# Attention and a gated feed-forward on one core: sums of exponentials on VectorE, turns of 32-bit pairs, and a new order for every engine

## The chip, the cores and the metric

The kernel runs on one NeuronCore of a Trainium2 chip. Five engines work on their own instruction queues, each in order: TensorE (PE in the profile, with its weight loads as PEld), VectorE (DVE), ScalarE (ACT), GpSimd (POOL) and SyncE (SP). In this kernel POOL only issues the loads and SP the stores. The metric is the device time of one launch in microseconds; less is better. The time before is 416.05 us, the median of three runs.

## The reference

Attention over 8 batches of 12 heads, 448 tokens, head size 64, and then a feed-forward with one gate over all 3584 tokens:

```
scores = (q @ k^T) / sqrt(64)                     # 8 x 12 x 448 x 448
attn   = softmax(scores)
x      = (attn @ v), heads side by side           # 3584 x 768
h      = x @ w_in                                 # 3584 x 2048
out    = (h * sigmoid(h)) @ w_out                 # 3584 x 768, float32
```

The inputs are float32 in memory; the loads turn them into fp16 on the way.

## The kernel before

**Units of attention.** Four heads make a group, three groups a batch. A unit is one group with a range of queries: batch 0 is cut into two pieces of queries (7 blocks of 32 each), so it has 6 units of 224 queries, and each later batch has 3 units of 448: 27 units. For each unit, `load_k`, `load_q` and `load_v` fetch fp16 tiles; `turn_k` (L265) and `turn_q` (L287) transpose 32x32 blocks on VectorE, so that 32 numbers of a head lie on 32 partitions. A head has 64 numbers, so there are two such halves (`e` = 0 and 1): the first and the last 32 numbers.

**Scores and exponentials.** The keys are cut into four chunks. `scores` (L315) makes one burst for one chunk: four heads work at the same time in four row strips of 32 of the array, and the two halves `e` add up in PSUM. `expo` (L335) makes exponentials on ScalarE, two heads at a time, into an fp16 tile `E`. The softmax has no subtraction of the maximum. The first seven units stand alone; the 20 others go in pairs, where the fourth chunk of both units has 64 keys each and shares one burst (`scores_rest`, L324) and one tile `E`.

**Columns.** `attend` (L364) multiplies the exponentials with V in four column strips of 32, one for each head, and it runs three times for a unit or a pair. Part 0 multiplies with `ones` and so gives the sums of the exponentials, that is, the denominators; parts 1 and 2 multiply with the first and the last 32 numbers of V. In a pair each part streams three chunks of each unit and then the shared fourth chunk. `inverse` (L387) turns the sums, takes reciprocals and turns them back, and `norm` (L403) multiplies and writes `xT`, the input of the feed-forward.

**Feed-forward.** `ffn1` (L420) multiplies `xT` with 16 blocks of w_in; `tanh` on ScalarE and `gate` (L464) on VectorE make the gated value (the sigmoid is had from the tanh of half the value). For the second product, two tiles of 128 tokens make a quad that is multiplied with seven products in place of eight; their inputs are sums of halves, made on VectorE by `combine_w` (L452) for the weights, once, and by `combine_g` (L489) for the tokens, in two halves of four blocks. `product` (L508) runs them, and `take_1` to `take_7` and `less_12`, `less_21` put the results together. The first two tiles of tokens are multiplied in the `plain` way (L524). `store` (L552) writes each output tile with four transfers, from SP, and a part of the last from ScalarE.

**What sets the order.** The program is written out by a planner in the kernel's own code: class `Order` (L76) keeps an estimated time and, for PE, ScalarE, VectorE and POOL, when each is free; every operation has an estimated length, dependencies and a bias. ScalarE and VectorE take the ready operation with the least sum of ready time and bias. PE's choice is made in the loop at L1082: a score burst when it is due (at most one per `PACE`, 2.6 us), else a column burst or a feed-forward product. Buffers are rings (`Ring`, L32): 2 score tiles of two PSUM banks, 4 other PSUM banks, 9 tiles `E`, 18 tiles `xT`, 6 output tiles and so on. `load` (L110) gives the loads in a fixed order; L652 to L677 list it. Until the first product, PE fills waits with multiplications of zeros (`run_zeros`, L1073). The estimates only set the order; on the chip every engine goes through its queue in that order and waits for what it needs.

Of the kernel before, what the change touches and what calls it, by code (L numbers as in the profile page):

```python
# [10 lines left out]
FP32 = mybir.dt.float32  # L11
AF = mybir.ActivationFunctionType
# [7 lines left out]
DMA_RATE = 0.37  # L20
DMA_TAIL = 1.0
# [54 lines left out]
class Order:  # L76


    def __init__(self):
        self.now = 0.0  # L80
        self.free = {"PE": 1.2, "ACT": 2.1, "DVE": 1.2, "POOL": 1.2}
        self.wait = {"ACT": [], "DVE": []}
        self.pool = []
        self.dma_free = 0.0
        self.out = []
        self.mode = None
        self.busy = {e: 0.0 for e in self.free}
# [22 lines left out]
    def load(self, mb, emit, ring=None, gate=None):  # L110
        op = Op("POOL", 0.58, emit)
        self.pool.append((op, mb, ring, gate))
        return op

    def step(self):

        soon = []
        for eng in ("ACT", "DVE"):
# [3 lines left out]
            best = None  # L122
            for op in self.wait[eng]:
                at = op.ready()
                if at is None:
                    continue
                if at > self.now:
                    soon.append(at)
                elif best is None or at + op.bias < best[0]:
                    best = (at + op.bias, op)  # L130
            if best:
                self.wait[eng].remove(best[1])
                self.start(best[1])
                soon.append(self.free[eng])
        if self.free["POOL"] > self.now:
            soon.append(self.free["POOL"])
        elif self.pool:
            op, mb, ring, gate = self.pool[0]
# [3 lines left out]
            if at is not None and gate is not None:  # L142
                g = gate()
                at = None if g is None else max(at, g)
            if at is not None and at <= self.now:
# [4 lines left out]
                self.dma_free = max(self.dma_free, self.now + 1.5) + mb / DMA_RATE  # L150
                op.done = self.dma_free + DMA_TAIL
                soon.append(self.free["POOL"])
# [6 lines left out]
def kernel(  # L159
# [31 lines left out]
    NE, NXT = 9, 18  # L191
    NSG, NTMP, NOST = 3, 3, 6
# [24 lines left out]
    pS_t = {}  # L217
# [4 lines left out]
    def load_k(b, hg):  # L222
        t = sb.tile([128, TPP, 2, 32], FP16, name=f"rk_{b}_{hg}", tag="rk", bufs=2)
        nc.gpsimd.dma_start(out=t, in_=group_of(k, b, hg))  # L224
        rawk[(b, hg)] = t

    def load_q(n):
        b, hg, g0, g1 = units[n]
        t = sb.tile([128, g1 - g0, 2, 32], FP16, name=f"rq_{n}", tag="rq", bufs=3)
# [21 lines left out]
    def load_w_in(h, j, f0, f1):  # L251
        src = moe_w_in.rearrange("(c h j p) f -> h j p c f", h=HG, j=2, p=32)
        dst = w_in_t.rearrange("p (c j) f -> p j c f", j=2)
        nc.gpsimd.dma_start(  # L254
            out=dst[32 * h : 32 * (h + 1), j, :, f0:f1], in_=src[h, j, :, :, f0:f1]
# [9 lines left out]
    def turn_k(b, hg, e):  # L265
        t = rawk[(b, hg)]
        if e == 0:
            KT[(b, hg)] = sb.tile(
                [128, 2, NCH, 4, 32], FP16, name=f"KT_{b}_{hg}", tag="KT", bufs=3
            )  # L270
        kt = KT[(b, hg)]
        toks = X_TOK[form(b, hg)]
        x = 0
        while x < 4:
            first, count = toks[x]
            y = x + 1
            while y < 4 and toks[y][1] == count:
                y += 1
            nc.vector.transpose(  # L279
                out=kt[:, e].rearrange("p c x i -> p x c i")[:, x:y, 0:count],  # L280
                in_=t[:, first : first + count * (y - x), e, :].rearrange(
# [5 lines left out]
    def turn_q(n):  # L287
        b, hg, g0, g1 = units[n]
        qt = sb.tile([128, 2, g1 - g0, 32], FP16, name=f"QT_{n}", tag="QT", bufs=3)
        nc.vector.transpose(out=qt.rearrange("p e g i -> p g e i"), in_=rawq[n])  # L290
        QT[n] = qt
# [7 lines left out]
    def score(pS, n, c, e, h, x0, x1, p0):  # L299
# [5 lines left out]
            lhsT=KT[(b, hg)][32 * h : 32 * (h + 1), e, c, x0:x1, :],  # L305
            rhs=QT[n][32 * h : 32 * (h + 1), e],
# [41 lines left out]
    def attend_mm(a, n, part, c, h, k0, k1, e, start, stop):  # L348
# [5 lines left out]
        else:  # L354
            w = VT[b][k0:k1, HG * hg + h, c, 32 * (part - 1) : 32 * part]
# [8 lines left out]
    def attend(ns, part):  # L364
        made = []
        lone = len(ns) == 1
        for n in ns:
            a = ps.tile([128, 512], FP32, name=f"a_{n}_{part}", tag="m", bufs=4)
            made.append(a)
            acc[(n, part)] = a  # L370
            for c in range(NCH if lone else NCH - 1):
                for h in range(HG):
                    attend_mm(
                        a, n, part, c, h, 0, rows_of(n, c), E[(n, c // per_burst(n))],
                        c == 0, lone and c == NCH - 1,
                    )
        if not lone:
            for h in range(HG):
                for i, n in enumerate(ns):
                    attend_mm(  # L380
                        made[i], n, part, 3, h, 64 * i, 64 * (i + 1), E[(ns[0], 3)],
                        False, True,
                    )


# [138 lines left out]
    def plain(t, j):  # L524
        o = ps.tile([128, 512], FP32, name=f"o_{t}_{j}", tag="m", bufs=4)
        pr_t[("o", t, j)] = o
        for f in range(NFF):
# [81 lines left out]
    s_ring, m_ring, e_ring = Ring(2), Ring(4), Ring(NE)  # L609
    rk_ring, rq_ring, v_ring = Ring(2), Ring(3), Ring(2)  # L610
    kt_ring, qt_ring = Ring(3), Ring(3)
    ld_k, ld_q, ld_v, ld_win, ld_wout = {}, {}, {}, {}, {}
    kt_op, qt_op, exp_op, rdn_op, x_op, g_op = {}, {}, {}, {}, {}, {}
    last_unit = {(u[0], u[1]): n for n, u in enumerate(units)}
    MB = 1e-6 * 4 * 32 * HG * D

    def plan_k(b, hg):
        ld_k[(b, hg)] = od.load(1.2 * MB * TPP, lambda: load_k(b, hg), rk_ring)

    def plan_q(n):  # L620
        ld_q[n] = od.load(1.2 * MB * (units[n][3] - units[n][2]), lambda: load_q(n), rq_ring)

    def plan_v(b, hg0, hg1):
        made = []
        for x in range(4):
            ring = v_ring if (x == 0 and hg0 == 0) else None
            mb = MB * (hg1 - hg0) * X_TOK[form(b, hg0)][x][1]
            made.append(od.load(mb, lambda x=x: load_v(b, hg0, hg1, x), ring))
# [3 lines left out]
    def plan_w_in(f0, f1):  # L632
        made = [
            od.load(4e-6 * 96 * (f1 - f0), lambda h=h, j=j: load_w_in(h, j, f0, f1))
            for h in range(HG)
            for j in range(2)
# [4 lines left out]
    def plan_w_out(half):  # L641
        made = []
        for f in range(0, NFF, 4):
            made.append(
                od.load(
                    4e-6 * 512 * OH,
# [5 lines left out]
    for hg in range(NG):  # L652
        plan_k(0, hg)
        plan_q(hg)
    plan_v(0, 0, NG)
    NB0 = NG * len(PIECES)
    for n in range(NG, 2 * NG):
        plan_q(n)
    plan_w_in(0, DFF // 4)
    for n in range(2 * NG, NB0):  # L660
        plan_q(n)
    plan_w_in(DFF // 4, DFF // 2)
    plan_k(1, 0)
    plan_q(NB0)
    plan_w_in(DFF // 2, DFF)
    plan_k(1, 1)
    plan_q(NB0 + 1)
    plan_w_out(0)
    plan_k(1, 2)
    plan_q(NB0 + 2)  # L670
    for hg in range(NG):
        plan_v(1, hg, hg + 1)
    plan_w_out(1)
# [15 lines left out]
    def plan_turn(n):  # L689
        b, hg, g0, g1 = units[n]  # L690
        if (b, hg) not in kt_op:
# [3 lines left out]
            for e in range(2):  # L695
                op = Op("DVE", 0.72, lambda e=e: turn_k(b, hg, e), [ld_k[(b, hg)]], 20)
                if e == 1:
                    op.then = rk_ring.give
                kt_op[(b, hg)] = od.add(op)
        if not qt_ring.can(1, od.now):  # L700
            return False
        qt_ring.take()
        busy = 0.1 + (g1 - g0) * 64 / 960.0
        qt_op[n] = od.add(
            Op("DVE", busy, lambda: turn_q(n), [ld_q[n]], 20, then=rq_ring.give)
# [8 lines left out]
    inv_op, norm_op = [], []  # L714
    quads = []

    def queue_ffn1(b, g0, g1):
        t0, t1 = 32 * g0, 32 * g1
        for f in range(NFF) if b == 0 else [x for f in range(HF) for x in (f, f + HF)]:

            def run(f=f):
                op = Op("PE", NDC * mm(t1 - t0), lambda: ffn1(b, f, t0, t1), tail=PE_OUT)
                if warm["on"]:
# [5 lines left out]
                    Op("ACT", act(t1 - t0), lambda: tanh(b, f, t0, t1), [op], -0.3, tail=0.2)  # L729
# [6 lines left out]
                    -4,  # L736
                    then=m_ring.give,
                )
                g_op.setdefault((b, f), []).append(od.add(g))
                ffn1_left[b] -= 1  # L740
# [17 lines left out]
    def sums_w(ms):  # L758

        for m in ms:  # L760
# [7 lines left out]
                        30,  # L768
# [5 lines left out]
    def queue_plain(t, j):  # L774
        def run():
            op = Op("PE", NFF * mm(OH), lambda: plain(t, j), tail=PE_OUT)
            m_ring.take()
            od.on_pe(op, "full")
            plain_op[(t, j)] = op
            od.add(  # L780
                Op("ACT", act(OH), lambda: take_plain(t, j), [op], -2, then=m_ring.give)
            )
            if len(plain_op) == 4:
                sums_w((3, 7))

        def deps():
            if any(len(g_op.get((0, f), ())) < len(PIECES) for f in range(NFF)):
                return [None]
            return ld_wout[j] + [(x, f * mm(OH)) for f in range(NFF) for x in g_op[(0, f)]]

        moe.append((deps, 1, run))
# [6 lines left out]
    def plan_sums():  # L798
# [12 lines left out]
        for m in (5, 2, 1, 6, 7):  # L811
            sg_op[(qd, m)] = []
            for f0 in (0, 4):
                deps = [x for f in range(f0, f0 + 4) for x in gates[f] + gates[f + HF]]
                if m > 5:
                    deps += sg_op[(qd, {6: 2, 7: 5}[m])]
                sg_op[(qd, m)].append(
                    od.add(
                        Op(
                            "DVE",  # L820
                            0.34,
                            lambda m=m, f0=f0: combine_g(qd, m, f0, f0 + 4),
                            deps,
                            0,
                        )
                    )
                )

    def queue_quad(qd):
# [3 lines left out]
        def read(m, eng, fn, deps, then=None):  # L833
            busy = act(OH) if eng == "ACT" else OH / 960.0 + 0.13
            bias = -2 if eng == "ACT" else -4
            took[m] = od.add(Op(eng, busy, lambda: fn(qd), deps, bias, then=then))

        def queue(m, first):
# [25 lines left out]
            def deps():  # L864
# [10 lines left out]
                x = sg_op.get((qd, m), [None, None])  # L875
                return made + [x[0], (x[1], 4 * mm(OH))]
# [47 lines left out]
    for ns in jobs:  # L924
        if len(ns) == 1:
            split = ((0,), (1,)) if ns[0] < 6 else ((0, 1),)
# [6 lines left out]
    av_data = {"at": None}  # L933

    def qk_at():
# [9 lines left out]
        if at is None or s is None or e is None:  # L945
            return None
        return max(at, s, e)

    def run_qk():
        ns, c, ys = qk_seq.pop(0)  # L950
        n = ns[0]
# [20 lines left out]
        for y in ys:  # L972
# [10 lines left out]
            for m in ns:  # L983
                exp_op.setdefault(m, []).append(made)
# [174 lines left out]
```

## Time and profile before

| | |
|---|---|
| runs | 414.36, 416.05 and 422.96 us; median 416.05 |
| span of the profiled execution | 414.8 us (the page gives no other time for it) |
| TensorE busy | 402.2 us, 97% of the span; granted clock 0.998 of full speed |
| weight loads, beside the matmuls | 208.0 us |
| VectorE, ScalarE busy | 285.2 us, 233.2 us |
| GpSimd busy (it issues the loads) | 95.8 us |
| moved by DMA | 34.46 MB |

An engine's busy time is the union of its instructions' times. Matmuls overlap, since the next one enters the array before the last one has left it, so one of 448 columns shows 353 ns where a row of them goes on every 0.188 us or so. In the chain that ended last, pieces are merged: "x12" are twelve matmuls, and the number before the engine is the time that they took on the chain. In a list of waits the three numbers are the total in us, how often, and the longest. In a list of groups the numbers after the count are the busy time in us and the mean of one in ns, and then the idle time before them and what ended it.

### The profile page before, as it was taken

Reading aid. Unit: us, or ns where it says so; the run is one execution under the profiler, and the core shown is the slowest. Engines: PE = TensorE matmul, PEld = TensorE weight load, DVE = VectorE, ACT = ScalarE, POOL = GpSimd, SP = SyncE. Lnnn points to the kernel's source line nnn. Section 1 sums busy time; section 2 is a strip of 40 time slices with the busy share of each in tenths; the row PEclk is TensorE's granted clock in tenths of the full one; section 3 lists DMA queues with packets and bytes.
Section 4 is the critical chain, followed back from the end, with each engine's and each line's share of the span. In section 5 each row is a group of like instructions: output and inputs, shape, how many; then the busy total and the mean of one; then the engine's idle time right before and its main releaser. Section 6 shows DMA issues by size and latency. Waiting matters only on the chain.

```text
span 414.8 us, 9788 instructions
## 1 busy us (share of the span) xinstructions
PE 402.2 (97%) x3939; PEld 208.0 (50%) x3939; DVE 285.2 (69%) x654; ACT 233.2 (56%) x360; POOL 95.8 (23%) x175
## 2 busy tenths in 40 slices
PE   8999999899999999999999899999999999999994
PEld 8676765344454445544445444444445444555562
DVE  3556765899868477867868838949577557684763
ACT  2987884587365794058476197476683373314410
POOL 6685374723000810053100071403000000000000
PEclk9999999999999999999999999999999999999999
DMA  6999999954313960284402294365002300032014
GB/s 102 147 169 193 203 131 210 197 79 69 50 40 92 128 92 14 60 135 77 73 3 57 72 154 72 35 109 92 1 6 51 81 19 2 22 81 54 0 45 108
DMA packets 38749, 34.46 MB, mean 83 GB/s; under 512 B 11952, under 2 KB 37936, under 8 KB 38704
## 3 DMA queue, kind: packets, MB, share of 16 engines
q0 software_dynamic: 27952, 22.82, 38.2%
q1 hardware_dynamic: 10560, 10.83, 10.3%
q8 instruction: 31, 0.51, 0.5%
q10 hardware_dynamic: 192, 0.20, 0.2%
q14 instruction: 14, 0.11, 0.1%
HBM read 45.61 MB, written 11.01 MB: 136 GB/s over the span
## 4 chain that ended last, share of the span: by engine, by line
PE 79%; DMA 10%; DVE 6%; POOL 3%; issue 1%; ACT 0%; DVEq 0%
PE h L423 32%; PE p L514 27%; PE a L356 10%; PE s L303 8%; DMA rq<-in_q_dram 6%; DMA rk<-in_k_dram 3%; PE z L1077 2%; DMA w_in_t<-in_moe_w_in_dram 1%; POOL w_in_t L254 1%; DVE sT L392 1%; DVE KT L279 1%; POOL V L243 1%; DVE QT L290 1%; DVE rdn L401 1%; DVE xT L409 1%
## 5 line engine op out<-in xcount | busy, mean ns | idle before, releaser
L340 ACT ACTIVATE E<-s 128x896 f16<-128x896 f32 (+1 forms) x172 | 148.4, 914 | 54.3 <-PE s L303 53.3
L423 PE MATMUL h<-xT,w_in_t 128*128 128x448 f16 (+1 forms) x864 | 157.5, 333 | 2.5 <-DVE xT L409 1.5
L423 PEld LDWEIGHTS <-w_in_t 128*128 128x128 f16 x864 | 79.1, 98 | 75.8 <-issue 22.0
L470 DVE SCALAR_TENSOR_TENSOR G<-th,h 128x448 f16<-128x448 f16 (+2 forms) x144 | 74.9, 530 | 55.6 <-ACT th L434 52.6
L434 ACT ACTIVATE th<-h 128x448 f16<-128x448 f32 (+1 forms) x144 | 71.5, 506 | 55.6 <-PE h L423 47.3
L243 POOL DMA_DIRECT2D V<-in_v_dram x88 | 48.6, 564 | 127.6 <-PE a L356 108.5
L303 PE MATMUL s<-QT,KT 32*128 32x448 f16 (+4 forms) x864 | 54.3, 334 | 1.7 <-ACT E L340 1.1
L514 PEld LDWEIGHTS <-G 128*128 128x128 f16 x384 | 36.5, 98 | 29.3 <-issue 5.7
L514 PEld LDWEIGHTS <-S 128*128 128x128 f16 x312 | 29.3, 98 | 23.2 <-issue 4.3
L356 PE MATMUL a<-E,V 128*32 128x448 f16 (+3 forms) x864 | 40.5, 335 | 0.0
L279 DVE STREAM_TRANSPOSE KT<-rk 128x256 f16<-128x256 f16 (+2 forms) x96 | 31.6, 377 | 12.0 <-DMA rk<-in_k_dram 10.3
L514 PE MATMUL p<-D,G 128*128 128x384 f16 x208 | 37.8, 327 | 0.0
L514 PE MATMUL p<-w_out_t,S 128*128 128x384 f16 x208 | 37.0, 327 | 0.2 <-DVE S L504 0.2
L409 DVE SCALAR_TENSOR_TENSOR xT<-a,rdn 128x448 f16<-128x448 f32 (+1 forms) x54 | 28.7, 563 | 11.1 <-PE a L356 10.8
L514 PE MATMUL p<-w_out_t,G 128*128 128x384 f16 x176 | 31.8, 327 | 1.2 <-DVE m L567 1.2
L303 PEld LDWEIGHTS <-KT 32*128 32x128 f16 (+2 forms) x864 | 17.3, 98 | 28.2 <-issue 26.9
L504 DVE TENSOR_TENSOR S<-G 128x512 f16<-128x512 f16 x70 | 25.7, 416 | 5.5 <-PE p L514 5.4
L356 PEld LDWEIGHTS <-V 128*32 128x32 f16 (+2 forms) x864 | 17.9, 95 | 22.7 <-issue 14.7
L290 DVE STREAM_TRANSPOSE QT<-rq 128x896 f16<-128x896 f16 (+1 forms) x27 | 26.5, 983 | 0.1
L224 POOL DMA_DIRECT2D rk<-in_k_dram x24 | 13.6, 566 | 51.2 <-DVE KT L279 47.6
L577 ACT COPY ost<-p 128x384 f32<-128x384 f32 x13 | 6.2, 480 | 29.3 <-PE p L514 29.3
L392 DVE STREAM_TRANSPOSE sT<-a 128x448 f32<-128x448 f32 (+1 forms) x27 | 15.6, 579 | 9.6 <-PE a L356 9.6
(38 smaller groups left out, 252.0 us busy)
## 6 DMA issues: line engine op xcount, KB each, us to landing
out_dram<-ost SPq DMA_DIRECT2D x220, 48.0 KB, 1.6
rk<-in_k_dram POOLq DMA_DIRECT2D x24, 224.0 KB, 5.3
rq<-in_q_dram POOLq DMA_DIRECT2D x21, 224.0 KB, 6.0
w_out_t<-in_moe_w_out_dram POOLq DMA_DIRECT2D x8, 384.0 KB, 9.9
V<-in_v_dram POOLq DMA_DIRECT2D x43, 64.0 KB, 4.2
V<-in_v_dram POOLq DMA_DIRECT2D x40, 48.0 KB, 4.2
w_in_t<-in_moe_w_in_dram POOLq DMA_DIRECT2D x16, 96.0 KB, 4.7
w_in_t<-in_moe_w_in_dram POOLq DMA_DIRECT2D x8, 192.0 KB, 6.9
```

The source lines that it names most:

```text
L243: nc.gpsimd.dma_start(out=VT[b][32 * x : 32 * (x + 1), hs, 0:count, :], in_=v[b, hs].rearrange("h (i g) d -> i h g d", g=TPP)[:, :, first ...
L279: nc.vector.transpose(out=kt[:, e].rearrange("p c x i -> p x c i")[:, x:y, 0:count], in_=t[:, first : first + count * (y - x), e, :].rearr ...
L290: nc.vector.transpose(out=qt.rearrange("p e g i -> p g e i"), in_=rawq[n])
L303: nc.tensor.matmul(out=pS[p0 : p0 + 32 * (x1 - x0), h % 2, at : at + nq], lhsT=KT[(b, hg)][32 * h : 32 * (h + 1), e, c, x0:x1, :], rhs=QT[ ...
L340: nc.scalar.activation(out=E[(n, w)][0:kr, 2 * y : 2 * y + 2, 0:nk], in_=pS_t[(n, w, y)][0:kr, :, 0:nk], func=AF.Exp, scale=attn_scale,)
L356: nc.tensor.matmul(out=a[32 * h : 32 * (h + 1), 0:nq], lhsT=w, rhs=e[k0:k1, h, at : at + nq], start=start, stop=stop,)
L409: nc.vector.scalar_tensor_tensor(out=xT[(b, cc)][:, 32 * g0 : 32 * g1], in0=acc[(n, part)][:, 0:nq], scalar=0.5, in1=rdn_t[n].rearrange("p ...
L423: nc.tensor.matmul(out=h[:, 0 : t1 - t0], lhsT=w_in_t[:, cc, 128 * f : 128 * (f + 1)], rhs=xT[(b, cc)][:, t0:t1], start=(cc == 0), stop=(c ...
L434: nc.scalar.activation(out=th, in_=h_t[(b, f, t0)][:, 0 : t1 - t0], func=AF.Tanh)
L470: nc.vector.scalar_tensor_tensor(out=dst[:, f, at + lo : at + hi], in0=th_t[(b, f, t0)][:, lo - t0 : hi - t0], scalar=1.0, in1=h_t[(b, f, ...
L504: nc.vector.tensor_tensor(out=dst[:, f0:f1], in0=x[:, f0:f1], in1=y[:, f0:f1], op=op)
L514: nc.tensor.matmul(out=pr_t[(qd, BANK[m])][:, 0:OH], lhsT=w[:, f, :], rhs=W_[m][:, f, :], start=(f == 0 and BANK[m] == m), stop=(f == HF - 1),
```

## The change

Seven things change together.

1. **Sums of exponentials.** For the 20 units in pairs, VectorE adds the exponentials of the first three chunks into an fp16 tile `ES` (`add_exp`): chunk 0 and 1, then chunk 2, in two halves of two heads each, four instructions a unit. Part 0 of `attend` then multiplies `ones` with `ES` once, in place of three times with `E`. There are two tiles `ES`.
2. **Pairs.** Q and K are turned as 32-bit words, two neighbouring fp16 numbers at a time. One turn does what two did; the two halves are now the even and the odd numbers of a head, so the scores read K and Q at every second element, V's weights are taken at every second column, and w_in's rows are loaded to match.
3. **w_in** comes in 12 transfers of 256 rows by 512 columns, over all 128 partitions, in place of 24 over 32 partitions.
4. **Joined bursts.** In batch 0, where a score burst had two heads, it takes four if both score tiles are free.
5. **Column bursts back to back.** Where the array is still in the shape of the shared chunk, the next column burst of a pair begins with that chunk.
6. **Rings and sizes.** `E` 9 to 10, `xT` 18 to 12, output tiles 6 to 4; the K tile of batch 0's last group and three Q tiles of batch 0 borrow buffers of `S` and of the output. The sums of tokens (`combine_g`) are made in one instruction in place of two, and the plain product is queued in four pieces.
7. **Order.** The planner gets a table `P` of biases and waits, other estimates for loads, an order of loads as a text, and rules for a hold before due bursts and for operations that wait for a more urgent one.

```diff
+    pace0=2.9, pace=3.11, half=0.45, av_wait=0.3, av_wait0=0.59, av_chain=3, hold=0.05, ahead=4,
...
+    loads=(
+        "k0.0 q0 k0.1 q1 k0.2 v0.0.3 q2 q3 q6 q4 i0.4 i8.12 k1.0 q5 "
+        "i4.8 v1.0.1 i12.16 k1.1 o0 q7 k1.2 q8 v1.1.2 o1 v1.2.3 "
...
-    NE, NXT = 9, 18
-    NSG, NTMP, NOST = 3, 3, 6
+    NE, NXT, NES = 10, 12, 2
+    NSG, NTMP, NOST = 3, 3, 4
...
-    def load_w_in(h, j, f0, f1):
-        src = moe_w_in.rearrange("(c h j p) f -> h j p c f", h=HG, j=2, p=32)
...
+    def load_w_in(c, f0, f1):
         nc.gpsimd.dma_start(
+            out=w_in_t[:, 2 * c : 2 * c + 2, f0:f1],
+            in_=moe_w_in[256 * c : 256 * (c + 1), f0:f1].rearrange("(p j) f -> p j f", j=2),
...
-        qt = sb.tile([128, 2, g1 - g0, 32], FP16, name=f"QT_{n}", tag="QT", bufs=3)
-        nc.vector.transpose(out=qt.rearrange("p e g i -> p g e i"), in_=rawq[n])
-        QT[n] = qt
+        qt = sb.tile([128, g1 - g0, D], FP16, name=f"QT_{n}", tag="QT", bufs=NQT)
+        nc.vector.transpose(out=qt.bitcast(PAIR), in_=rawq[n].bitcast(PAIR))
+        QT[n] = qt.rearrange("p g (i e) -> p g i e", e=2)
...
-            lhsT=KT[(b, hg)][32 * h : 32 * (h + 1), e, c, x0:x1, :],
-            rhs=QT[n][32 * h : 32 * (h + 1), e],
+            lhsT=KT[(b, hg)][32 * h : 32 * (h + 1), c, x0:x1, :, e],
+            rhs=QT[n][32 * h : 32 * (h + 1), :, :, e],
...
-            w = VT[b][k0:k1, HG * hg + h, c, 32 * (part - 1) : 32 * part]
+            w = VT[b][k0:k1, HG * hg + h, c, part - 1 :: 2]
...
+    def add_exp(n, w, y):
+        es = slice(2 * y, 2 * y + 2)
+        if w == 1:
+            if n not in ES:
+                ES[n] = sb.tile([128, HG, S], FP16, name=f"ES_{n}", tag="ES", bufs=NES)
+            first = E[(n, 0)]
+        else:
+            first = ES[n]
+        nc.vector.tensor_tensor(
+            out=ES[n][:, es], in0=first[:, es], in1=E[(n, w)][:, es], op=ALU.add
+        )
...
+        if early and not lone:
+            rest(True)
+        for n in ns:
+            a = made[n]
+            if part == 0 and n in ES:
+                for h in range(HG):
+                    attend_mm(a, n, 0, 0, h, 0, 128, ES[n], not early, early)
+                continue
...
+        if ys == (0,) and s_ring.can(2, od.now):
+            qk_seq.pop(0)
+            ys = (0, 1)
...
-            for f0 in (0, 4):
...
+                    Op("DVE", 0.6, lambda m=m: combine_g(qd, m, 0, HF), deps, P["b_sum"])
```

## The prediction

> **What bounds the kernel now.** I read the engines' shares first, then the stretches, then the chain and what TensorE (PE) waited for.
>
> ```profile
> PE 402.2 (97%) x3939; PEld 208.0 (50%) x3939; DVE 285.2 (69%) x654; ACT 233.2 (56%) x360; POOL 95.8 (23%) x175
> ```
>
> PE is never free for long, but "busy" joins overlapping matmuls, so it says nothing yet of useful work. The stretches (columns: length, busy time of PE, its weight loads, VectorE (DVE), ScalarE (ACT), GpSimd (POOL)) split the run:
>
> ```profile
> 0.00:36.00 36.00, 33.40 (x595) 25.74 (x599) 19.41 (x55) 23.51 (x31) 24.05 (x47) 1.00 0.98 145
> 36.00:80.00 44.00, 42.88 (x532) 26.16 (x525) 28.91 (x71) 31.79 (x57) 23.84 (x42) 1.00 1.19 186
> 80.00:354.00 274.00, 270.81 (x2495) 124.68 (x2496) 200.25 (x449) 162.92 (x244) 47.88 (x88) 1.00 0.38 65
> 354.00:415.00 61.00, 55.09 (x323) 31.37 (x321) 36.67 (x81) 14.97 (x29) 0.00 (x0) 0.98 0.21 53
> ```
>
> To 36 us batch 0's attention runs, thinly; from 36 to 409 PE works without a pause, attention among the two products to 354, products alone after it. DVE has 73% in the long stretch. Two pieces of the chain and PE's waits show what PE's time is made of there:
>
> ```profile
> 104.57 2.38 PE h L423 x12
> 109.55 1.56 PE a L356 x32
> 112.51 0.49 PE s L303 x8
> 113.00 2.71 PE p L514 x16
> ```
> ```profile
> PE h L423 <- DVE xT L409: 1.5, 2, 1.2
> PE p L514 <- DVE m L567: 1.2, 1, 1.2
> PE s L303 <- ACT E L340: 1.1, 3, 0.4
> ```
>
> Six h matmuls without a change of array shape take 1.13 (a piece of the same chain), so 448 columns stream in 0.188 us. A column burst for a pair of units is 7 streams (3 chunks of each, and the shared fourth), 1.32 of its 1.56; the rest, like the 0.11 in h's 2.38 and in s's 0.49 (two streams are 0.38), is the cost of changing shape. PE's waits of all kinds sum to under 8 us. After 36 us the time therefore falls by what is taken out of PE's stream, and by little else.
>
> **The change, part by part.**
>
> *Sums of exponentials.* Of 27 units the first 7 are alone, 20 go in 10 pairs. In part 0 (the denominators, against ones) each unit of a pair had 3 streams and has one; the shared chunk stays. That is 2 x 2 x 0.188 = 0.754 us a pair, **7.5 us** in all, every pair lying after 68 us, where PE has no slack. The price is 80 additions on DVE (20 units, two chunks, two halves) of 896 fp16 numbers. The nearest rows:
>
> ```profile
> L504 DVE TENSOR_TENSOR S<-G 128x512 f16<-128x512 f16 x70 | 25.7, 416 | 5.5 <-PE p L514 5.4
> L460 DVE TENSOR_TENSOR D<-w_out_t 128x1536 f16<-128x1536 f16 x6 | 5.6, 942 | 4.7 <-DMA w_out_t<-in_moe_w_out_dram 4.7
> L290 DVE STREAM_TRANSPOSE QT<-rq 128x896 f16<-128x896 f16 x21 | 22.8, 1087 | 0.1
> L401 DVE STREAM_TRANSPOSE rdn<-inv 128x448 f32<-128x448 f32 x21 | 13.1, 623 | 0.1
> ```
>
> Slope 0.514 ns an element gives 613 ns for 896; three of 512 in a row take 1.09, so 0.08 of each overlaps, and one adds 0.533: 42.6 us. They do not delay the denominators: the last addition of a pair can run under the shared chunk's two exponentials (1.73 us in the timeline). An addition waits in DVE's queue for its ACTIVATE, and its tile for the matmuls of two units before; behind it stand gates (each gives back one of four PSUM banks) and norms.
>
> *Turning as 32-bit pairs.* The row of the fp32 turn has 448 elements in 623 ns, against 1087 for 896 halves: 21 Q turns save 0.464 each, six small ones (0.616 to 0.41) 0.2, and of 96 K turns (36.3 us by shape) half go: 9.8 + 1.2 + 18.2 = 29 us of DVE. No row turns 32-bit integers in SBUF outright; the bounds are 0 (they cost by half-words) and 29. I take 29, the fp32 row being nearest. With half-sized sums merged (65 pairs of 2 x 0.337 to one of 0.60: 5 us) DVE goes from 200 to about 200 - 17 (its turns) - 3.4 + 40 = 220 of 274, 80%. Covered by PE; without the cover, see the first rival.
>
> The scores now read K and Q at every second element, and V's weights likewise. No row has a strided matmul operand. Bounds: nothing (streams as now), and each score stream twice as long, 28 us (70 pair bursts and 4 of unit 6, 0.378 each). I take nothing, since all PE rows, whatever their row and column counts, keep one pace; the other end is a rival. The Trainium skill ("SBUF — State Buffer", Door 1) says SBUF is read at full bandwidth if a 16-byte line is hit at least twice; every second fp16 hits it four times, so by the page the price is nothing; no run here shows it yet.
>
> *Joined bursts.* Batch 0's score bursts of two heads become four heads when both banks are free. That saves PE time, but before 36 us, where ACT is the limit:
>
> ```profile
> 9.40:36.00 26.60, 20.75 (x24) 1.00 1.09 163
> ```
>
> These are batch 0's 24 exponentials on ACT; with 6 tanh of 1.78 it idled 4.1 of 26.6 us. Joining gives two exponentials per burst but leaves both banks busy between: from a loss of 1 to a gain of 4, I take 1.
>
> *First burst.*
>
> ```profile
> 1.03 7.93 PE L1077 MATMUL z<-zeros 128*128 128x128 f16 x91 [1.03 <-DVE zeros L207]
> 6.22 0.60 DVE L290 STREAM_TRANSPOSE QT<-rq 128x448 f16<-128x448 f16 x1
> ```
>
> Q is turned at 6.82, yet scores start at 8.9, behind 91 zeros in PE's queue, 87 ns each. The new turns are 0.8 shorter (K 1.29 to 0.70, Q 0.60 to 0.41), and so is the row of zeros: 0 to 2.1, I take 1. **Start: 2.0 us** together.
>
> *Loads.* w_in goes from 24 issues to 12: 12 x 0.564 = 6.8 us less on POOL, which was busy 24 of the first 36. Q and K of batch 1 pass w_in parts in the new order. The transfers fill the queues to 80 us (share 1.19 in the second stretch), bytes stay, so I price it at nothing: the start is ACT's, and after 36 PE already streams. If K comes late DVE blocks on it: 1.2 us of PE's wait on xT at 81 us was such a case. Without the cover the most is 10.3 us, all that DVE waits for K's transfers now; a gain can't exceed the 2 us that PE loses between 36 and 80 us beside shape changes.
>
> *Order and rings.* A column burst that follows another may begin with the shared chunk and save one change of shape, 0.11 to 0.13. At most four of nine changes a pair go, 10 x 4 x 0.11 = 4.4; at the least none. In the old chain only a few column bursts stand back to back, so I take **1.0**. PE's waits after 80 us (3 to 4 us) can go or grow as the order is new: **1.0** off. Tiles for x 18 to 12 (two batches): batch 3's first V burst, at 132, would wait for batch 1's h, done by 107, cover 25 us. Output tiles 6 to 4: SP issues a tile's four stores in 1.86 us, landing 1.6 later, while products alone give a tile per 2.3: four tiles last 9. Nothing, at worst 1.9 at the end. The plain product in four pieces changes no shape: nothing.
>
> The Trainium skill ("SBUF — State Buffer", Who interferes with whom) has a rule against the additions: with two SBUF inputs they lock GpSimd's SBUF reads out. The row of POOL's issues has 562 to 566 ns for K, Q and V alike, and such an issue beside the old sums was no longer; by the rule 80 x 0.61 = 49 us of POOL at most, which idles 226 of 274. The sum stays.
>
> **Sum**: 414.8 - 7.5 - 2.0 - 1.0 - 1.0 = 403.3 of span. The page has no other time of the profiled execution; the median of the three runs, 416.05, lies 1.25 above the span, and I carry that: **404.5**.
>
> **Rivals.**
>
> 1. *VectorE gives it back.* If 32-bit turns save nothing, DVE has 237 of 274 (86%); and even at 80% gates wait behind additions. For (same columns as above):
>
> ```profile
> 80.00:100.00 20.00, 18.52 (x157) 7.67 (x158) 19.72 (x45) 15.81 (x24) 8.58 (x16) 1.00 0.64 96
> ```
>
> Here DVE was busy 19.72 of 20, and PE lost 1.48. Over 274 us that rate would be 20; at the lower load I take 40% of it, 8: **412**, range 408 to 416. Against: four banks allow 4.5 us of h while one needs about 2.5.
> 2. *The strided score reads stream at half pace*: 28 us on PE's path, **432**, slower than before. Place: every L303 burst. It decides from a stream 41% longer (11.5 of 28), and makes it over 2% slower from 71%. Against: the readings so far show one element per beat for all shapes.
> 3. *More at the start and in the order*: all 2.1 of the zeros, 4 of ACT's idle, 4.4 of changes: 6.5 to 7.5 beyond what I took, **397**.
> 4. *The additions do not relieve PE*: if the streams against ones ran beside something else, part 0 would not shorten on the chain. The chain shows 1.56 for it as for V, so I give this nothing of its own.
>
> **How the numbers follow.** Forecast 404.5 (399 to 408) 0.58; VectorE 0.20; half pace 0.12; more 0.10. The range 395 to 416 leaves out half pace and some of the last. A measurement of this kernel tells about 2%, 8.3 us: faster is below 407.7. Faster 0.58 + 0.10 = 0.68; within 2% 0.20; slower 0.12.
>
> **What would show it.** The a-E,ones matmuls fall from 248 of 448 columns to about 88 plus the shared ones; a part-0 burst takes 0.8 in the chain; s bursts stay 0.49 (rival 2: 0.87); L290 turns near 0.62; the new additions near 0.6; DVE near 80% from 80 to 350; first scores near 8; last product near 398. The forecast is wrong if PE's waits on DVE grow past 8 us, or if stores or late loads hold it up.

## The result and the profile after

The changed kernel takes **401.27 us** (median of 4 runs, 399.95 to 408.51); the kernel before took 417.11 us beside it (median of 4). The ratio is **0.964**, 95% interval 0.957 to 0.971: faster. The forecast was 404.5, range 395 to 416. In some runs of most kernels, before and the changed one (408.51) included, the granted clock is lower (0.50 from 20 to 30 us in the six that were profiled) and some 6 to 9 us are added; the ratios, and the means of runs below, leave those out, except in experiment 9, where all runs are of this kind.

The profiled run took 400.96 us with a span of 399.1, 15.7 less than the 414.8 of before. The engines' shares of the changed kernel (busy us, share of the span, instructions):

```profile
PE 390.3 (98%) x3745; PEld 200.7 (50%) x3745; DVE 304.8 (76%) x621; ACT 234.8 (59%) x360; POOL 90.9 (23%) x163
```

Its stretches (length, then busy time of PE, weight loads, VectorE, ScalarE, GpSimd, the clock granted to PE, DMA's share, GB/s):

```profile
0.00:36.00 36.00, 33.70 (x606) 25.55 (x607) 17.78 (x52) 25.49 (x36) 24.23 (x43) 1.00 1.13 175
36.00:80.00 44.00, 43.23 (x504) 24.79 (x504) 36.38 (x81) 34.73 (x60) 22.28 (x40) 1.00 1.13 179
80.00:354.00 274.00, 274.00 (x2413) 128.36 (x2412) 225.52 (x446) 162.95 (x244) 44.41 (x82) 1.00 0.37 65
354.00:399.00 45.00, 39.38 (x227) 21.96 (x225) 25.09 (x43) 11.59 (x22) 0.00 (x0) 0.96 0.23 56
```

From 80 to 354 us PE is busy in all of the 274 us (before: 270.81), and VectorE in 225.52, 82% (before 200.25; the prediction had 220). What PE still waits for is little, and after 80 us nothing of it is left:

```profile
PE s L352 <- DVE QT L339: 1.7, 2, 1.0
PE z L1199 <- DVE zeros L251: 1.0, 1, 1.0
PE s L352 <- ACT E L389: 0.3, 1, 0.3
```

A piece of the chain that ended last (start, us, engine, line, matmuls merged):

```profile
99.86 2.38 PE h L495 x12
102.24 0.51 PE s L352 x8
102.74 2.71 PE p L586 x16
...
110.61 0.81 PE a L405 x16
111.41 0.51 PE s L352 x8
111.92 2.71 PE p L586 x16
```

A part-0 burst takes 0.81 where the old chain had 1.56; h and p take what they took. A score burst takes 0.51, not 0.49. The groups behind VectorE's edits, and the new denominators (count, busy us, mean ns, idle time before and what ended it):

```profile
L421 DVE TENSOR_TENSOR ES<-E,E 128x896 f16<-128x896 f16 x40 | 24.3, 614 | 10.2 <-ACT E L389 10.2
L421 DVE TENSOR_TENSOR ES<-ES,E 128x896 f16<-128x896 f16 x40 | 24.2, 620 | 2.5 <-ACT E L389 2.3
L339 DVE STREAM_TRANSPOSE QT<-rq 128x448 int32<-128x448 int32 x21 | 13.1, 624 | 2.7 <-DMA rq<-in_q_dram 2.7
L405 PE MATMUL a<-ES,ones 128*32 128x448 f16 x80 | 5.6, 358 | 0.0
```

The additions take 614 to 620 ns, the Q turns 624 (before 1087). And the start, from the timeline of PE (start, us, ..., count, what it waited for): 60 zeros in place of 91, and the first scores at 7.05 where they came at 8.9.

```profile
1.03 6.08 PE L1199 MATMUL z<-zeros 128*128 128x128 f16 x60 [1.03 <-DVE zeros L251]
...
7.05 0.58 PE L352 MATMUL s<-QT,KT 32*128 32x224 f16 x16
```

**Where the 15.7 us come from.** I add up the streams of all matmuls but the zeros (columns at 0.188 us for 448; four column or row strips at a time count once, eight for the shared chunk) and call the rest of the time lost to PE.

| us | before | after | difference |
|---|---|---|---|
| streams of PE, whole run | 352.85 | 345.33 | -7.5 |
| lost to 36 us | 22.3 | 19.4 | -2.9 |
| lost from 36 to 80 us | 6.6 | 5.8 | -0.8 |
| lost from 80 us to the end | 33.1 | 28.7 | -4.4 |
| span | 414.8 | 399.1 | -15.7 |

The streams fell by what the prediction took out. The other half of the gain is lost time that went away, and there it had 4.0. After 36 us the changes of shape fell from 225 to 211; at 0.11 to 0.13 that is 1.5 to 1.8 of the 5.3, and the rest is waits and gaps.

### The profile page after: what moved, and what is told of

Read it like the earlier page. It is cut to its first block, busy times and chain, and to the rows that moved or that the text cites. A ratio compares the mean times of both kernels' runs of the same rounds, so it can differ in the third digit from the quotient of the medians.

```text
span 399.1 us, 9369 instructions
## 1 busy us (share of the span) xinstructions
PE 390.3 (98%) x3745; PEld 200.7 (50%) x3745; DVE 304.8 (76%) x621; ACT 234.8 (59%) x360; POOL 90.9 (23%) x163
## 4 chain that ended last, share of the span: by engine, by line
PE 90%; DMA 5%; POOL 2%; DVE 1%; issue 0%; POOLq 0%
PE h L495 35%; PE p L586 30%; PE a L405 12%; PE s L352 11%; DMA rq<-in_q_dram 5%; PE o L601 3%; POOL w_out_t L310 1%; POOL V L295 1%; POOL rk L272 1%; POOL rq L282 0%; DVE QT L339 0%; DVE ost L640 0%; PE z L1199 0%; DVE sT L464 0%; POOLq L1269 0%
## 5 line engine op out<-in xcount | busy, mean ns | idle before, releaser
L495 PE MATMUL h<-xT,w_in_t 128*128 128x448 f16 (+1 forms) x864 | 154.9, 332 | 0.0
L495 PEld LDWEIGHTS <-w_in_t 128*128 128x128 f16 x864 | 80.0, 98 | 71.1 <-issue 16.8
L542 DVE SCALAR_TENSOR_TENSOR G<-th,h 128x448 f16<-128x448 f16 (+2 forms) x144 | 76.0, 535 | 32.3 <-ACT th L506 30.2
L405 PE MATMUL a<-E,V 128*32 128x448 f16 (+3 forms) x864 | 39.3, 334 | 0.0
L421 DVE TENSOR_TENSOR ES<-E,E 128x896 f16<-128x896 f16 x40 | 24.3, 614 | 10.2 <-ACT E L389 10.2
L352 PEld LDWEIGHTS <-KT 32*128 32x128 f16 (+2 forms) x864 | 16.4, 98 | 29.3 <-issue 26.2
L421 DVE TENSOR_TENSOR ES<-ES,E 128x896 f16<-128x896 f16 x40 | 24.2, 620 | 2.5 <-ACT E L389 2.3
L576 DVE TENSOR_TENSOR S<-G 128x1024 f16<-128x1024 f16 x35 | 22.1, 683 | 0.1
L328 DVE STREAM_TRANSPOSE KT<-rk 128x256 int32<-128x256 int32 (+3 forms) x48 | 16.5, 382 | 6.6 <-DMA rk<-in_k_dram 6.5
```

The costliest lines, as they stand in the source:

```text
L352: nc.tensor.matmul(out=pS[p0 : p0 + 32 * (x1 - x0), h % 2, at : at + nq], lhsT=KT[(b, hg)][32 * h : 32 * (h + 1), c, x0:x1, :, e], rhs=QT[ ...
L405: nc.tensor.matmul(out=a[32 * h : 32 * (h + 1), 0:nq], lhsT=w, rhs=e[k0:k1, h, at : at + nq], start=start, stop=stop,)
L421: nc.vector.tensor_tensor(out=ES[n][:, es], in0=first[:, es], in1=E[(n, w)][:, es], op=ALU.add)
L495: nc.tensor.matmul(out=h[:, 0 : t1 - t0], lhsT=w_in_t[:, cc, 128 * f : 128 * (f + 1)], rhs=xT[(b, cc)][:, t0:t1], start=(cc == 0), stop=(c ...
L542: nc.vector.scalar_tensor_tensor(out=dst[:, f, at + lo : at + hi], in0=th_t[(b, f, t0)][:, lo - t0 : hi - t0], scalar=1.0, in1=h_t[(b, f, ...
L576: nc.vector.tensor_tensor(out=dst[:, f0:f1], in0=x[:, f0:f1], in1=y[:, f0:f1], op=op)
```

## The experiments

Each mean is over 3 to 10 runs. The runs came in three sets, in which before had means of 416.1, 415.6 and 416.9 us; beside the changed kernel (400.8) it had 416.2. The ratio is against before in the same set. In the last column a difference of 1 to 2 us is little more than what before differs between sets. Not undone alone were the new transfers of w_in, the sizes of the rings and the merged sums of tokens.

| kernel | mean, us | ratio (95% interval) | against the changed kernel, us |
|---|---|---|---|
| changed kernel | 400.8 | 0.964 (0.957 to 0.971) | |
| without the sums | 408.5 | 0.982 (0.978 to 0.986) | +7.7 |
| 16-bit turns, planned anew | 410.9 | 0.988 (0.984 to 0.992) | +10.1 |
| 32-bit turns in that order | 411.8 | 0.991 (0.987 to 0.994) | +11.0 |
| 16-bit turns in the changed kernel's order | 408.3 | 0.982 (0.978 to 0.985) | +7.4 |
| old rules and biases | 412.3 | 0.990 (0.986 to 0.995) | +11.5 |
| old pace alone | 401.2 | 0.965 (0.962 to 0.969) | +0.4 |
| plain product in one piece | 412.6 | 0.989 (0.982 to 0.997) | +11.8 |
| old order of loads | 402.9 | 0.967 (0.959 to 0.974) | +2.1 |
| no joined bursts, no shared chunk first | 402.7 | 0.969 (0.965 to 0.973) | +1.8 |
| additions left out | 399.9 | 0.959 (0.952 to 0.966) | -0.9 |
| shorter start | 407.5 | 0.977 (0.972 to 0.983) | +6.7 |
| before, with the sums alone | 419.5 | 1.008 (1.005 to 1.011) | |

**1. The sums taken out.** Everything else of the change stays, but the planner, told the longer bursts, writes its own order.

```diff
-            if c in (1, 2) and form(*units[n][:2]) != "lone":
+            if False:
```

> The changed kernel, but part 0 streams the three chunks of E again and VectorE adds no exponentials. Theory (TensorE's stream is the time): 10 pairs get four streams of 0.188 us back, so the span grows by 7.5 us, from 399.1 to about 406.6, although VectorE is relieved of 48 us. Rival (the new order alone made the gain, the additions cost on VectorE what they save): the span stays at 399 or falls.

408.5, +7.7 us. The four streams of 0.188 per pair, 7.5 us in 10 pairs, come back one for one: the term of 7.5 is right, and so is that it lies on PE's path.

**2. The sums alone, on the kernel before** (with rings of 12 for `xT` and 4 for the output, which make room for `ES`).

> The kernel before with the additions of exponentials alone (and the changed sizes of the rings for x and the output, to make room); turns of 16-bit numbers, old order. Theory: 7.5 us less than before, span near 407. Rival (without the pairs VectorE, at 86 to 88 percent in the long stretch, gives it back): 412 to 416, and TensorE's waits on VectorE grow past 10 us.

Neither: 419.5, slower than before by 0.8%. PE's streams fell by the same 7.5, but the time lost to PE rose by 8.7. From 80 to 354 us VectorE has 235.72 of 274 us, 86%, and PE now waits for it (waits of this kernel: total us, times, longest):

```profile
PE h L439 <- DVE xT L425: 4.0, 3, 3.2
PE s L303 <- ACT E L340: 2.5, 5, 1.0
PE p L530 <- DVE xT L425: 1.5, 1, 1.5
```

So the sums by themselves are no gain here. They need room on VectorE, or an order that can bear it, and this run does not say which of the two, nor what the smaller rings cost it.

**3. The turns as 16-bit numbers.** Same layout of numbers (even and odd), two turns in place of one, and operands of the scores without a step. The planner is told the true lengths and so writes another order.

```diff
-            nc.vector.transpose(
-                out=kp.rearrange("p c x i -> p x c i")[:, x:y, 0:count],
+            for e in range(2):
+                nc.vector.transpose(
+                    out=kt[:, e].rearrange("p c x i -> p x c i")[:, x:y, 0:count],
...
-            rhs=QT[n][32 * h : 32 * (h + 1), :, :, e],
+            rhs=QT[n][32 * h : 32 * (h + 1), e],
```

> The changed kernel, but K and Q are turned as 16-bit numbers, the even and the odd ones apart, so the scores read without a step. Theory: VectorE gets about 29 us more (near 334 in all) and TensorE covers it: 0 to 3 us longer. Rival (VectorE is the next limit, and only the pairs make room for the additions): 8 us or more longer. If the stepped reads cost TensorE anything, score bursts get shorter than 0.49 us here.

410.9: the rival's size. But its loss is not spread over the run, as a VectorE that is too full would spread it. The stretch from 104 to 121 us of this kernel, and then of the changed one:

```profile
104.00:121.00 17.00, 12.98 (x136) 3.33 (x135) 15.04 (x27) 9.62 (x12) 1.73 (x4) 0.60 0.17 28
```
```profile
104.00:121.00 17.00, 17.00 (x149) 8.20 (x148) 15.92 (x32) 11.32 (x16) 0.00 (x0) 1.00 0.15 36
```

PE is busy in 12.98 of 17 us, at a granted clock of 0.60. PE's timeline there:

```profile
104.24 0.36 PE L355 MATMUL s<-QT,KT 32*128 32x448 f16 x2 [1.00 <-ACT E L392]
105.05 0.55 PE L355 MATMUL s<-QT,KT 32*128 32x448 f16 x6 [0.45 <-ACT E L392]
106.44 0.56 PE L355 MATMUL s<-QT,KT 32*128 32x448 f16 x2 [0.83 <-ACT E L392]
107.24 0.93 PE L355 MATMUL s<-QT,KT 32*128 32x448 f16 x6 [0.25 <-ACT E L392]
...
116.17 4.47 PE L408 MATMUL a<-E,V 128*32 128x448 f16 x64
120.57 0.56 PE L355 MATMUL s<-QT,KT 32*128 32x448 f16 x8
121.06 1.15 PE L589 MATMUL p<-w_out_t,G 128*128 128x384 f16 x6
```

No product is in PE's queue from 102 to 121 us: batch 1's h is done, and p comes at 121. PE has attention alone, which ScalarE paces, with an idle moment ahead of each half of a burst; from 107 on matmuls take 1.7 times as long besides (0.93 for six where it was 0.55). The products of a quad begin with one that reads a sum of w_out, made in two halves and written back into w_out's own tile. The planner lets VectorE make these sums when nothing else is ready (their bias is the largest of the table), and with longer turns it finds such a moment late. The second half, in this kernel and in the changed one (VectorE's timeline):

```profile
115.69 0.92 DVE L535 TENSOR_TENSOR w_out_t<-w_out_t 128x1536 f16<-128x1536 f16 x1
```
```profile
81.38 0.95 DVE L532 TENSOR_TENSOR w_out_t<-w_out_t 128x1536 f16<-128x1536 f16 x1
```

**4. The order and the work, taken apart.** First the changed kernel with its 32-bit turns but in the order of experiment 3, then the 16-bit turns in the changed kernel's order. In each only the length that the planner is told differs from its parent:

```diff
-            op = Op("DVE", 0.62, lambda: turn_k(b, hg), [ld_k[(b, hg)]], P["b_turn"])
+            op = Op("DVE", 1.24, lambda: turn_k(b, hg), [ld_k[(b, hg)]], P["b_turn"])
...
-        busy = 0.08 + (g1 - g0) * 32 / 960.0
+        busy = 0.08 + (g1 - g0) * 64 / 960.0
```

> The changed kernel with its 32-bit turns, but with every instruction of PE, ScalarE, the stores and the loads in the order of the run with 16-bit turns (the planner is told twice the turns' cost, nothing else). Theory O: the 10 us lost with 16-bit turns came from that order, which uses up the feed-forward products by 104 us and then has attention alone at ScalarE's pace; 408 to 412 us, with PE losing over 10 us from 100 to 150. Rival V: they came from VectorE's 22 us more of work; then this takes 401 to 403 and the hole is gone.

411.8, as experiment 3, with 22 us less for VectorE to do (305.9 us busy against 327.6). Its hole, at 106 to 127 us of a run of 417.84:

```profile
106.00:127.00 21.00, 16.03 (x169) 5.43 (x167) 18.18 (x37) 12.95 (x17) 2.41 (x5) 0.84 0.14 23
```

So the order alone is enough for that loss, and in that order the turns' length is worth nothing.

> The changed kernel's own order on PE, ScalarE, the stores and the loads, with K and Q turned as 16-bit numbers (the planner is told the 32-bit turns' cost). VectorE has about 22 us more to do. Theory O: 401 to 403 us, no hole at 100 to 150. Rival V: 408 to 412, with PE waiting on VectorE for xT, QT or the gates.

408.3, +7.4: in the changed kernel's own order the turns' length does cost, and theory O falls for this half. VectorE goes from 225.52 to 234.60 of the 274 us, 86%, and PE from 274 to 267.32; there is no hole, but waits of all kinds on VectorE (the longest groups of them):

```profile
80.00:354.00 274.00, 267.32 (x2376) 123.91 (x2375) 234.60 (x471) 162.16 (x245) 46.48 (x85) 1.00 0.36 63
```
```profile
PE h L498 <- DVE G L545: 3.5, 3, 1.5
PE s L355 <- DVE QT L339: 2.3, 3, 1.6
PE p L589 <- DVE m L643: 1.2, 1, 1.2
PE h L498 <- DVE X L545: 1.2, 1, 1.2
```

The waits on VectorE sum to 9.9 us, against 1.7 in the changed kernel. Both causes are there, then, and each alone is enough to lose most of what they lose together.

This pair of kernels also prices the stepped operands, by the groups of the scores (changed kernel, then this one):

```profile
L352 PE MATMUL s<-QT,KT 32*128 32x448 f16 x496 | 35.6, 360 | 0.8 <-DVE QT L339 0.8
```
```profile
L355 PE MATMUL s<-QT,KT 32*128 32x448 f16 x496 | 34.5, 353 | 2.1 <-DVE QT L339 2.1
```

7 ns a matmul, 0.02 a burst (0.51 against 0.49): with 70 pair bursts and 4 of unit 6 about 1.5 us, not 28.

**5. Is there room left on VectorE?** The changed kernel's order with the 80 additions left out, so that two of the first three chunks are missing from the denominators of the units in pairs.

```diff
-        nc.vector.tensor_tensor(
-            out=ES[n][:, es], in0=first[:, es], in1=E[(n, w)][:, es], op=ALU.add
-        )
+        ES[n] = E[(n, 0)]
```

> The changed kernel's own order on every engine, but the 80 additions are left out: the denominators of a paired unit are taken from its first chunk's exponentials alone and the shared chunk's (so part of the sum is missing). VectorE has about 43 us less to do, PE's stream is unchanged. Theory: from 80 to 354 us PE is busy all the time as it is, so the additions cost PE nothing; 400 to 401.5 us. Rival: VectorE at 82% still delays gates and norms; then 397 to 399.5.

399.9, 0.9 us less, a little below the theory's interval and above the rival's. VectorE falls to 69% of the long stretch and PE's busy time cannot rise:

```profile
80.00:354.00 274.00, 274.00 (x2427) 127.32 (x2424) 189.21 (x378) 166.29 (x249) 48.11 (x88) 1.00 0.38 65
```

So with VectorE at 82% the additions cost about 1 us at most, which lies within the spread of the changed kernel's runs (399.95 to 401.58); with the turns that take VectorE to 86% the loss is 7.4.

**6. The order's rules.** All numbers of the planner's table set back as far as the old kernel had them (pace 2.6, no holds, the old biases, the plain product in one piece). The table's lines are joined here, and some are left out.

```diff
-    pace0=2.9, pace=3.11, av_wait=0.3, av_wait0=0.59, av_chain=3, hold=0.05, ahead=4,
+    pace0=2.6, pace=2.6, av_wait=0.0, av_wait0=0.0, av_chain=99, hold=-1.0, ahead=3,
-    b_turn=40, b_comb=52.81, b_sum=-10, b_es=10, b_norm=-3.29, b_gate=-20, lazy=0.34, plain=4,
+    b_turn=20, b_comb=30, b_sum=0, b_es=-4, b_norm=-10, b_gate=-4, lazy=0.0, plain=1,
...
```

> The changed kernel with the old pace (2.6 us), the old biases, and without the new holds and waits; sums, pairs, rings and loads stay as changed. Theory: the sums' 7.5 us and the start's 2 to 3 stay, and the shape changes and waits that the order saved (5.5 us after 36 us by the two traces) come back: 403 to 405 of span. Rival (the order matters little): 399 to 401.

412.3, more than either. The loss is again in one place:

```profile
122.00:141.00 19.00, 14.77 (x154) 4.70 (x156) 12.91 (x26) 10.44 (x13) 1.21 (x3) 0.73 0.11 27
```

Here the products of two quads, which follow batch 1's h, are used up at 122 us, before batch 2's attention is complete. Counting matmuls shows why: at 120 us the changed kernel has issued 440 score matmuls, this one 384.

> The changed kernel with one number of the planner set back: a score burst is due every 2.6 us, not every 2.9 (batch 0) and 3.11. Theory: this number alone uses up the feed-forward products too early, so a stretch comes in which PE has only attention at ScalarE's pace; 408 to 413 us, PE losing over 10 us in one stretch of 50. Rival: the holds and biases of the new order made the difference, and the pace alone gives 401 to 403.

One number of that table, the pace, set back alone gives 401.2: as the changed kernel. My theory that the pace makes the hole falls.

> The changed kernel with the plain product planned in one piece of 16 matmuls again, not in four. The prediction priced the four pieces at nothing: then 400 to 402 us. Theory: between the end of batch 1's first product and the start of batch 2's PE has a stock of products for about 26 us only; a coarser piece lets batch 2's attention come late, and PE runs dry for 5 to 10 us between 100 and 150; 407 to 412.

Another one, the plain product in one piece, gives 412.6, with a like hole at 118 to 136 us:

```profile
118.00:136.00 18.00, 13.04 (x157) 3.73 (x160) 13.53 (x27) 11.65 (x14) 0.00 (x0) 0.73 0.12 28
```

At 120 us it has issued 376 score matmuls and has no p left. That this one setting decides in this order is shown; that it is the setting that decides among the old rules is not, since others of them were not tried alone. How it decides is open: at 85 us the two kernels are one burst of scores apart (336 and 328 matmuls), but the columns of the next pair, which start at 88.47 us in the changed kernel, start at 112.58 here, and from 95 to 110 us no score is issued.

**7. Joined bursts and the shared chunk first.** Both branches off.

```diff
-        if ys == (0,) and s_ring.can(2, od.now):
+        if False:
...
-        early = od.mode == "rest cols"
+        early = False
```

> The changed kernel without joined score bursts in batch 0 and without column bursts that begin with the shared chunk. The prediction's terms for these two were 1.0 and 1.0; the traces of before and after have 225 and 211 changes of shape after 36 us, 1.8 us. Expected 402.5 to 404.5 us, half of it before 36 us. Rival: bursts are joined only where ScalarE sets the pace and the order finds the same room otherwise; then 401.3 as the changed kernel.

402.7, +1.8, within what was expected. Its lost time to 36 us is 20.4 against 19.4, and after that it loses 0.6 more: the two terms of 1.0 hold, nearly in size and in place. The two branches were not switched off one by one.

**8. The order of loads.**

```diff
-        "k0.0 q0 k0.1 q1 k0.2 v0.0.3 q2 q3 q6 q4 i0.4 i8.12 k1.0 q5 "
+        "k0.0 q0 k0.1 q1 k0.2 q2 v0.0.3 q3 q4 q5 i0.4 i4.8 k1.0 q6 "
...
```

> The changed kernel with the list of loads in an order near the old one (Q of unit 2 ahead of V, w_in in order, K and Q of batch 1 before V of batch 1). The prediction priced the order of loads at nothing: 400 to 402.5. Rival: the new order is what brings batch 2's attention in time; then over 405, with PE running dry between 100 and 150.

402.9, +2.1: slightly above what a price of nothing allows, far from the rival.

**9. A shorter start, tried as an improvement.** The first 12 zeros left out, and Q of unit 2 ahead of the first V.

```diff
+        cut = min(n, warm.get("cut", 12))
+        n, warm["cut"] = n - cut, warm.get("cut", 12) - cut
...
+    todo.remove(q2)
+    todo.insert(todo.index(v0), q2)
```

> An improvement of the changed kernel at the start, every other instruction in its order: 12 zero matmuls fewer in PE's first row (1.2 us, for Q is turned at 5.8 and scores start at 7.05), and Q of unit 2 loaded ahead of the first V. Theory: the start's savings carry to the end, as the 2.9 us that the change itself saved before 36 us did; 0.5 to 1.5 us less, 399.3 to 400.3 us. Rival: ScalarE and the transfers take them up before 36 us; then as the changed kernel.

407.5, and all six runs between 406.6 and 409.4: slower. The scores do start earlier, at 6.29, but the first burst on V can't: V's transfers are issued 0.5 to 0.6 us later (4.6 to 6.4 us, against 4.0 to 5.9) and take up to 8.4 us to land (7.7), and PE now stands idle for 2.04 us ahead of that burst (the profile names no releaser). From PE's timeline and from the stretches (the clock is third from the end):

```profile
14.93 1.34 PE L405 MATMUL a<-E,V 128*32 128x224 f16 x32 [2.04 <-issue]
```
```profile
12.00:20.00 8.00, 5.95 (x102) 3.73 (x99) 2.64 (x8) 3.86 (x6) 5.33 (x9) 0.71 1.29 203
20.00:37.00 17.00, 17.00 (x217) 10.18 (x210) 6.43 (x19) 9.42 (x13) 10.98 (x18) 0.53 1.25 203
```

The same stretches of the changed kernel:

```profile
12.00:20.00 8.00, 7.01 (x155) 4.66 (x154) 4.02 (x12) 6.09 (x8) 5.70 (x9) 1.00 1.27 203
20.00:37.00 17.00, 17.00 (x330) 12.64 (x323) 11.26 (x32) 14.95 (x24) 10.60 (x18) 1.00 1.24 198
```

The clock granted is 0.53 from 20 to 37 us and PE gets through 217 matmuls in place of 330. The mean clock of all six runs is 0.972 to 0.977, where three of the changed kernel's four have 0.996 or 0.997, so the loss lies in the clock; what the edits would be worth without it is not shown. Which of the two opened the wait was not tried apart. What it says of the start: V's landing bounds it (the changed kernel's first burst on V starts at 13.65 us), not the zeros, and here it did not help to be at the wait sooner.

## Why the prediction was right, and where its steps were not

**Direction and size.** 404.5 was said, 401.27 came, and faster by more than 2%, as the likeliest case had it. The profiled span fell by 15.7 where the sum had 11.5. The terms of the sum that missed, the start and the order, were too small. One part of the hit is luck: that the new order leaves no stretch in which PE runs out of products was not worked out, and the neighbouring orders of experiments 3, 4 and 6 that do cost 10 to 12 us.

**The sums, 7.5: right.** The streams fell by 7.5 and taking them out cost 7.7. "After 36 us the time therefore falls by what is taken out of PE's stream, and by little else" is right for its first half only: 5.3 us of lost time went away too.

**Start, 2.0: too small by a third.** It was 2.9. The zeros went from 91 to 60 and the scores from 8.9 to 7.05, 1.85 where 1 was taken and 2.1 stood as the upper end; the other 1.0 is the joined bursts (experiment 7).

**Order, 1.0 and 1.0: mis-sized.** Shape changes gave 1.5 to 1.8, near the first term; PE's waits and gaps after 36 us some 3.5 where the second term had 1.0, since almost every wait went. The text knew that these waits "can go or grow"; the runs with other orders show how much they can grow: up to 11.8.

**"Covered by PE": right for the additions, wrong for the turns.** Leaving out the 80 additions is worth 0.9. But the 29 us of turns were counted as a relief for an engine that is covered anyway, hence nothing; undone in the same order they cost 7.4. The condition and price stood in the first rival, "If 32-bit turns save nothing, DVE has 237 of 274 (86%)", 8 us: the run had 234.6 of 274, 86%, and 7.4. The rival had mechanism, place and price, though the price was 40%, by choice, of a rate read from 20 us of the old kernel, so that it came this close is partly luck. What kept it from coming was that 32-bit turns do take the fp32 turn's time, 624 ns.

**"The plain product in four pieces changes no shape: nothing": wrong by 11.8.** It changes no shape, but in this planner it decides whether batch 2's attention comes in time (experiment 6; by what steps is not shown). The reasoning priced the edit by what it does to PE's stream and not by what comes late through it.

**Order of loads, nothing: nearly.** 2.1. The 12 transfers of w_in take POOL 707 ns each to issue, not 564, so POOL is relieved of 4.9 us (95.8 to 90.9) and not of 6.8; no term of the sum rested on it.

**The stepped operands, nothing: nearly.** 1.5 us. The Trainium skill ("SBUF — State Buffer", Door 1) gave nothing as well, since a line of 16 bytes is hit four times; the 0.02 us a burst is what the trace has beside it. Rival 2, 28 us, is refuted.

**The additions against GpSimd.** The Trainium skill's rule that a VectorE operation with two SBUF inputs contends with a GpSimd instruction that reads SBUF ("SBUF — State Buffer", Who interferes with whom) shows no price here: with 80 such additions POOL's issues for V take 563 ns on average, for K 565, for Q 561, as before (564, 566 and 563).

**The parts do not add up.** Sums 7.7, turns 7.4, rules 11.5, loads 2.1 and bursts 1.8 make 30, and the whole is worth about 15 (416.2 to 400.8). My reading is that the sums fill VectorE, the turns make room on it, and the order spends PE's stock of products evenly, so that with any one missing what the others bring is partly lost.

## What to carry to other kernels

The same engine off the critical path, at 82% and at 86%, was 7 us apart here: price a relief on it by undoing it in the new kernel, not by the old kernel's cover. Where PE lives on a stock of products between two phases, look at how much there is and when the next phase is ready; a run that fell short by 10 us for this did not wait here and there but stood in one hole, which a table by stretch shows at once. And when a part is undone, hold the order of the engines fixed, or the new order's luck is measured with it.

## What the hardware did that I had not expected

- **The granted clock fell after PE had gaps, and PE's work then took up to 1.7 times as long.** With idle moments of 1.00, 0.45, 0.83 and 0.25 us in a row (experiment 3) six score matmuls went from 0.55 to 0.93 us, 64 column matmuls from about 3.07 to 4.47, until products came back; one gap of 2.04 us (experiment 9) was followed by a clock of 0.53 from 20 to 37 us. So a hole costs more than its idle time: in experiment 3 PE was idle for 4.0 of the 17 us, and the loss was some 10. At the start the two went together in all fourteen profiles: where PE stood idle ahead of its first burst on V for 1.17, 1.18, 1.58, 1.62, 2.04 or 2.56 us, at about 13 us, the clock was 0.50 from 20 to 30 us; in the other eight, whose longest gap from 9 to 20 us was 0.96 or less, it stayed at 1.00.
- **32-bit integer words turn at the pace of fp32**: 448 words in 624 ns, where 896 halves took 1087.
- **A step of two in a matmul's operands** leaves the stream's pace as it is and adds 7 ns to a matmul (353 to 360 ns).
